# Splitting the opening of an FFT-mixing and GEGLU kernel by residue parity

## Chip, cores, metric

The kernel runs on one core of a Trainium2 chip. The metric is the device time of one execution in microseconds (us), as the median of the runs; lower is better.

## The reference

The input x has 8 batches of 3008 tokens with 256 channels. The first half takes the real part of a two-dimensional Fourier transform over tokens and channels; the second is a gated feed-forward layer with 1536 hidden columns:

```
X = np.fft.fft(x, axis=1); X = np.fft.fft(X, axis=2); a = X.real
g = a @ w_gate                                  # (24064, 1536)
out = (0.5*g*(1 + erf(g/sqrt(2))) * (a @ w_val)) @ w_out   # (24064, 256)
```

## The kernel before

**The transform.** 3008 tokens are 64 x 47. The first stage (`a_step`, 12 steps a batch) multiplies the folded input `xf` by a table `G` of 64-point cosines and sines and copies the result from PSUM to `S1`; its rows are residues. `z_write` puts `S1` into a DRAM tile `z`, `z_read` brings it back as `Ap` with another layout, in three thirds. The second stage (`b_steps`) multiplies 32 slices of `Ap` by 47-point tables (`TP`, `TQ`, and `T0P`, `T0Q` for residue 0) in four groups `q` of eight, once for the even half of the channel transform (`eo` = 0) and once for the odd one (`eo` = 1). `evac` copies a group from PSUM into the token columns `Y`: 1505 columns a batch, since the transform's symmetry gives the other 1503 rows. For batch 0 the odd half runs each step a second time with a one-column weight (`m1`).

The channel transform is folded into the weights: `gen_w` multiplies `w_gate` and `w_val`, cast to bf16 by `cast_w` on POOL, by the table `CW` and copies out `WE`, `WOP` and `WOM` (the odd half with the sign of the mirrored rows). `CW` comes from `phase_c` (POOL), `reduce_c` (DVE) and `sin_c` (ACT).

**Units.** A batch's columns go in three chunks, `CH = [(1024, 481), (0, 512), (512, 512)]`, and each chunk in 12 units of 128 hidden columns: 36 units a batch, 288 in all. A unit multiplies its chunk of `Y` by gate and value weights, for plus and minus rows, applies Gelu on ACT (`glp`, `glm`) and forms the products `h` on DVE (and POOL). In the first chunk of batch 0 (`kind` 0) a unit has six matmuls; from unit 12 on it has five, and DVE makes the minus rows from a broadcast row `nq`, which `n_first` (batch 0) or `n_step` provides. When a chunk's 12 units are done, `l2_steps` multiplies `h` by `Wo_sb` and stores the rows, eight matmuls a unit, beside the next chunk's units.

**Order.** Everything is issued by one loop over units, in program order on each engine's own queue. Inside unit `u` PE runs `val_even(u)`, `gate_minus(u-1)`, `gate_plus(u)` and `val_odd(u-1)`; between them `fill()` pops two matmuls at a time from a list of second-stage steps. DVE's `plus` and minus products follow, then `tail()` empties the second-stage group. After that come the unit's extras (`extra`: `cast_w`, `gen_w`, `gen_wn`), the folds of the next batches on POOL, and the `a_step`s of the next batch (`a_first`: units 4, 5, 8 to 13 for batch 1).

**PSUM.** Of eight banks `ps_g` has two, `ps_v` two pairs, `ps_o` one and `ps_d` one. A new user of `ps_d` waits until the last one's copy is done. `ps_vh` gives half of a `ps_v` pair. In the loop `ps_d` serves `b_steps` of later batches, most `a_step`s, `gen_wn` and some `gen_w`.

**Queues.** All loads, z transfers and stores go through SP's queue in program order; only `load_wo` is on POOL's. In the opening SP has x of batch 0, the first third of the weights, z of batch 0, a small transfer `gate` from z, then the weights for units 4 to 7, x of batch 1 and the weights for units 8 to 11. `warm(n)` issues n matmuls that nothing reads, into `ps_d`; the last eight before the second stage take `gate` as weight, so they start when it lands.

Of the kernel before, what the change touches and what calls it, by code (L numbers as in the profile page):

```python
# [37 lines left out]
def kernel(  # L38
# [34 lines left out]
    CH = [(1024, NCOL - 1024), (0, 512), (512, 512)]  # L73
    MID = 24
# [26 lines left out]
    lone = const_pool.tile([128, NFC], BF16)  # L101

# [92 lines left out]
    def z_tile():  # L195
        return dram.tile([HJ, 128, C], BF16, tag="z", bufs=2, name="z")
# [139 lines left out]
    def sin_g(i):  # L336
        for h in range(2):
            act.activation(
                _sub(G, [[128, 8], [1, 64]], i * 8 * 128 + h * 64),
                _sub(reds[i], [[64, 8], [1, 64]], 0), AF.Sin, scale=col_h[h][:, :])  # L340

    def turn_g():
        for r, to, of, n, sign in ((0, 0, 0, 16, 1.0), (2, 2, 2, 16, -1.0), (1, 1, 33, 8, 1.0),
                                   (1, 33, 1, 8, -1.0), (3, 3, 35, 8, -1.0), (3, 35, 3, 8, 1.0)):
            pat = [[128, 8], [64, 2], [4, n]]
            act.activation(_sub(G, pat, 16 * 128 + to), _sub(G, pat, of), AF.Copy, scale=sign)
# [32 lines left out]
    def reduce_c():  # L379
        for both in redc:  # L380
            reduce_phase(both[:, :C], both[:, C : 2 * C])
        vec.tensor_scalar(col_m, col_p, 1.0, -2.0, op0=ALU.is_ge, op1=ALU.mult)
# [14 lines left out]
    def gen_w(f0, i, eo, bank):  # L397
        fs = slice(f0, f0 + 512)
        ps = bank()
        for t in range(NCH):  # L400
            on_half(ps, pe.matmul(
                ps, CW[:, t, eo, :], _sub(wb[(f0, i)], [[1, 512]], t * 512),
                start=(t == 0), stop=(t == NCH - 1)))
        if eo == 0:
            on_half(ps, act.activation(WE[:, i, fs], ps, AF.Copy))
        else:
            on_half(ps, act.activation(WOP[:, i, fs], ps, AF.Copy))
            on_half(ps, vec.tensor_scalar(
                WOM[:, i, fs], ps, col_m, None, op0=ALU.mult))

# [21 lines left out]
    def n_turn(b):  # L432
        pool.tensor_tensor(
            NA[:, :, :], _sub(Ap, [[0, 2], [C, NG]], 128), TB[:, :, :], op=ALU.mult)
# [46 lines left out]
    def z_write(b, j0, nj, eng=sync):  # L481
        if "z" not in st[b]:
            st[b]["z"] = z_tile()
        z, S1 = st[b]["z"], st[b]["S1"]
        dst = ap_replace(
            z[0:1, 0, :], ap=[[C, 128], [128 * C, nj], [1, C]], offset=z[j0, 0:1, :].offset)
        eng.dma_start(out=dst, in_=_sub(S1, [[C, nj], [1, C]], j0 * C))

    def z_read(b, third):
        z = st[b]["z"]  # L490
        src = ap_replace(
            z[0:1, 0, :], ap=[[NG * C, 32], [1, NG * C]], offset=z[8 * third, 0:1, :].offset)
        p_step = Ap[:, :, :].ap[0][0]
        dst = ap_replace(
            Ap[:, :, :], ap=[[4 * p_step, 32], [1, NG * C]],
            offset=Ap[:, :, :].offset + third * p_step)
        sync.dma_start(out=dst, in_=src)

    def b_steps(b, eo, q):

        box = {}

        def mm(gi, m1):
            def run():
                if "ps" not in box:
                    box["ps"] = ((ps_o, ps_d, ps_vh, ps_vh) if eo else (ps_vh, ps_g) * 2)[q]() \
                        if b == 0 else ps_d()
                ps = box["ps"]
                g = 8 * q + gi
                w = _sub(Ap, [[1, 1 if m1 else 128]], g * C + eo * 128)  # L510
                keep = lambda m: on_half(ps, m)
                even = m1 or eo == 0
                o = gi * N2
                r = slice(0, 1) if m1 else slice(0, 128)
                if g == 0:
                    t = T0P if even else T0Q
                    keep((pe.matmul(
                        ps[r, 0:N2], w, t[:, 0:N2], start=True, stop=True)))
                    keep(pe.matmul(ps[r, 8 * N2 : 8 * N2 + 1], w, t[:, N2 : N2 + 1],
                                         start=True, stop=True))  # L520
                else:
                    s = (36 * g) % N2
                    t = TP if even else TQ
                    keep(pe.matmul(
                        ps[r, o : o + N2], w, t[:, s : s + N2], start=True, stop=True))
            return run

        def copy(o, i):
            if b or q % 2:
                on_half(box["ps"], act.activation(o, i, AF.Copy))  # L530
            else:
                on_half(box["ps"], vec.tensor_copy(o, i))

        def evac_top():
            ps = box["ps"]
            if Ys[b] is None:
                Ys[b] = Y_tile()
            copy(
                _sub(Ys[b], [[32, MID], [1, 8]], eo * YW + 8 * q),
                _sub(ps, [[1, MID], [N2, 8]], 0))  # L540

        def evac_rest():
            if Ys[b] is None:
                Ys[b] = Y_tile()
            ps, Y, g0 = box["ps"], Ys[b], 8 * q
            n2 = N2 - MID
            f = 1 if q == 0 else 0
            copy(
                _sub(Y, [[32, n2], [1, 8 - f]], eo * YW + 32 * MID + g0 + f - 1),
                _sub(ps, [[1, n2], [N2, 8 - f]], MID + f * N2))  # L550
            if q == 0:
                copy(
                    _sub(Y, [[32, n2]], eo * YW + 32 * MID + 31), ps[:, MID:N2])
                copy(
                    _sub(Y, [[1, 1]], eo * YW + NCOL - 1), ps[:, 8 * N2 : 8 * N2 + 1])

        steps = [mm(gi, False) for gi in range(8)]
        if eo == 1 and b == 0:
            steps += [mm(gi, True) for gi in range(8)]
        def evac():  # L560
            evac_rest()
            evac_top()

        return steps, evac, evac_top, evac_rest


# [11 lines left out]
    def open_unit(u):  # L578
# [3 lines left out]
        c0, n = CH[ci]  # L582
# [82 lines left out]

    def windows(b, ci):
        h = hs[(b, ci)]
        c0, n = CH[ci]
# [8 lines left out]
        if len(blocks) % 4:  # L677
            left = blocks[-2:]
            o = 64 * (b % 2)
            pool.tensor_copy(hx[:, :, o : o + 64], h[:, :HXF, 896:960])  # L680
            pool.tensor_copy(_sub(CW, [[128, NCH * 2], [1, 64]], o), h[:, HXF:, 896:960])
            pool.tensor_copy(lone, h[:, :, 960:961])
            if b % 2:
                out.append((None, 0, st[b - 1]["left"] + left, None))
            else:
                st[b]["left"] = left
        return out

    def l2_steps(b, ci):
# [49 lines left out]

        def store_pair(pair, t, queues):  # L740
            ns = len(pair)
            for q in range(4):
# [23 lines left out]
    for i in (1, 0):  # L766
        load_w(0, i)
    phase_g(0)
    phase_g(1)
    cols_c()  # L770
# [3 lines left out]
    pool.tensor_copy(col_k, _sub(reds[1], [[1, 1]], 0))  # L774
    for i in range(3):
        fold_x(0, i, vec, other=pool)
        if i < 2:
            pool.memset(Ap[:, 16 * i : 16 * i + 16, :].bitcast(FP32), 0.0)
        else:
            for t in range(NCH):  # L780
                phase_c(t)
        for k in range(4 * i, 4 * i + 4):
            a_step(0, k)
            if i == 0 and k == 3:
                z_write(0, 0, 8)
            elif i and k % 2:
                z_write(0, 2 * k - 2, 4)
        warm((5, 2, 10)[i])
    z_read(0, 0)
    z_read(0, 1)  # L790
    gate = work.tile([128, 128], BF16, tag="gate", bufs=1, name="gate")
    sync.dma_start(out=gate[:, :], in_=ap_replace(
        st[0]["z"][0:1, 0, :], ap=[[C, 128], [1, 128]], offset=st[0]["z"][0:1, 0, :].offset))
    z_read(0, 2)
    for i in (1, 0):
        load_w(512, i)
    load_x(1, 0)
# [4 lines left out]
    reduce_c()  # L802
    cols_t()
    pt = phase_t()
    sin_c()
    cast_w(0)
# [3 lines left out]
    gen_w(0, 0, 0, ps_g)  # L810
    gen_w(0, 0, 1, ps_vh)
    act.activation(col_f[:, :], col_p[:, :], AF.Gelu)
    warm(4)
    warm(8, gate[:, :])
    later_evacs = []
    for eo in range(2):
        for q in range(4):
            steps, evac, evac_top, evac_rest = b_steps(0, eo, q)
            for s in steps:
                s()  # L820
            if eo:
                evac_rest()
                later_evacs.append(evac_top)
            else:
                evac()
    cast_w(512)
    load_wo()
    extra = {1: [lambda: cast_w(1024)], 13: [gen_tf]}
    for n, turn in ((0, (ps_o, ps_d, ps_o, ps_d)), (1, (ps_o, ps_o, ps_d, ps_o))):
        for j, bank in enumerate(turn):  # L830
            extra.setdefault(4 * n + j, []).append(
# [15 lines left out]
    plan = [first | evens, later | evens]  # L847
    l2q, few = [], False
    for u in range(NU + 2):
# [4 lines left out]
        if u < NU:  # L854
# [4 lines left out]
            if b + 1 < B:  # L859
                for what in plan[min(b, 1)].get(i, ()):  # L860
# [7 lines left out]
                    fills += st[b + 1]["cur"][0][lo:hi]  # L868
# [13 lines left out]
        if u == 0:  # L882
# [8 lines left out]
            n_first(0)  # L891
# [21 lines left out]
        if tail:  # L913
            tail()
        if 0 < u <= NU:
# [29 lines left out]
        if 0 < u <= NU and u % 12 == 0:  # L945
            pb, pi = divmod(u // 12 - 1, 3)
            if CH[pi][0] == 0:
# [34 lines left out]
```

## Time and profile before

| what | value |
|---|---|
| median of 3 runs | 631.36 us (629.62 to 632.13) |
| the profiled execution | 629.75 us |
| its span, first to last instruction | 627.6 us |
| TensorE busy (PE) | 606.0 us, 97% |
| weight loads (PEld), beside PE | 402.0 us, 64% |
| VectorE (DVE) / ScalarE (ACT) / GpSimd (POOL) | 86% / 75% / 72% |
| HBM traffic | 45.08 MB read, 37.25 MB written |

Busy time of PE is that of pipelined matmuls, whose ends are modelled. The waits are inferred from semaphores; the engine named is the one that came last. Line numbers in the profile are those of helpers, so groups are told apart by tile names: `h<-glp,ps_v` is the plus product, `Y<-ps_d` a copy of the second stage, `S<-ps_d` one of the first.

### The profile page before, as it was taken

The page shows a single profiled execution, that of the slowest core. Times are in us where ns is not written, and L with a number is a line of the kernel's source. Part 1 is how long each engine was busy: PE and PEld are TensorE (multiplying, and loading weights), DVE is VectorE, ACT ScalarE, POOL GpSimd, SP SyncE. Part 2 cuts the span into 40 slices and gives each one's busy share as a digit, 9 for nine tenths or more (in the row PEclk, how much of TensorE's full clock was granted, in tenths as well). Part 3 has the DMA queues.
Part 4 walks back from the last instruction along what each step waited for, and adds up shares of the span by engine and source line. Part 5 has one row for each costly group of instructions (what it writes and reads, how often), then busy time and mean ns, then how long its engine had stood idle before and what let it go on. Part 6 is the DMA issues. An engine that isn't in the chain of part 4 may idle for free.

```text
span 627.6 us, 12916 instructions
## 1 busy us (share of the span) xinstructions
PE 606.0 (97%) x4522; PEld 402.0 (64%) x4580; DVE 541.5 (86%) x654; ACT 471.8 (75%) x956; POOL 449.7 (72%) x480
## 2 busy tenths in 40 slices
PE   3899999999999999999999999999999999999997
PEld 2445666766666666766667666666667666666665
DVE  7688988898888998888988898889898898999991
ACT  8687778877788777877778777887778777766662
POOL 8296987769868789687787788687885555556552
PEclk9999999999999999999999999999999999999999
DMA  8997523653237512574246533366223612222113
GB/s 311 348 283 234 153 64 113 173 185 98 76 101 218 194 49 74 177 223 121 51 119 173 190 103 74 104 208 204 56 60 93 194 45 50 60 50 52 39 47 85
DMA packets 65458, 82.39 MB, mean 131 GB/s; under 512 B 8298, under 2 KB 58986, under 8 KB 62578
## 3 DMA queue, kind: packets, MB, share of 16 engines
q1 hardware_dynamic: 63682, 80.65, 42.4%
q0 software_dynamic: 1552, 0.79, 0.9%
q8 instruction: 36, 0.59, 0.4%
q14 instruction: 28, 0.23, 0.1%
q10 hardware_dynamic: 160, 0.13, 0.1%
HBM read 45.08 MB, written 37.25 MB: 131 GB/s over the span
## 4 chain that ended last, share of the span: by engine, by line
PE 91%; DMA 3%; DVE 3%; ACT 1%; issue 1%; POOL 0%; SPq 0%; ACTq 0%; DVEq 0%; POOLq 0%
PE ps_o L25 38%; PE ps_g L25 28%; PE ps_v L25 19%; PE ps_d L25 6%; DMA xin<-in_x_dram 3%; DVE h L25 1%; DVE S L25 0%; DMA z<-S 0%; ACT glp L25 0%; DVE xf L25 0%; ACT glm L25 0%; ACT S L25 0%; POOL xf L25 0%; SPq L25 0%; DVE WOM L25 0%
## 5 line engine op out<-in xcount | busy, mean ns | idle before, releaser
L25 POOL TENSOR_TENSOR h<-glm,dv 128x1024 bf16<-128x1024 bf16 (+1 forms) x138 | 290.9, 2108 | 153.2 <-DVE dv L25 110.0
L25 PE MATMUL ps_o<-Wo_sb,h 128*128 128x256 bf16 x2136 | 277.7, 272 | 0.5 <-DVE S L25 0.3
L25 DVE SCALAR_TENSOR_TENSOR ev<-nq,WN,ps_v 128x512 f32<-128x512 bf16 (+1 forms) x276 | 202.6, 734 | 62.3 <-PE ps_v L25 43.5
L25 ACT ACTIVATE glm<-ps_g 128x512 bf16<-128x512 f32 (+1 forms) x288 | 169.4, 588 | 110.0 <-PE ps_g L25 70.8
L25 PEld LDWEIGHTS <-h 128*128 128x128 bf16 x2208 | 210.8, 97 | 54.6 <-issue 0.9
L25 ACT ACTIVATE glp<-ps_g 128x512 bf16<-128x512 f32 (+1 forms) x288 | 169.9, 590 | 9.9 <-PE ps_g L25 0.3
L25 DVE TENSOR_TENSOR h<-glp,ps_v 128x1024 bf16<-128x1024 bf16 (+2 forms) x150 | 172.9, 1153 | 4.9 <-ACT glp L25 2.7
L25 DVE SCALAR_TENSOR_TENSOR dv<-ev,ps_v 128x1024 f32<-128x1024 f32 (+1 forms) x138 | 164.8, 1194 | 0.0
L25 POOL TENSOR_TENSOR xf<-xin 128x254 bf16<-128x254 f32 x168 | 118.3, 726 | 1.8 <-DMA xin<-in_x_dram 1.8
L25 PE MATMUL ps_g<-Y,WOM 128*128 128x512 bf16 (+1 forms) x288 | 107.7, 374 | 0.3
L25 PE MATMUL ps_v<-Y,WOP 128*128 128x512 bf16 (+1 forms) x288 | 107.7, 374 | 0.0
L25 PE MATMUL ps_v<-Y,WE 128*128 128x512 bf16 (+1 forms) x282 | 105.7, 375 | 0.1
L25 PE MATMUL ps_g<-Y,WOP 128*128 128x512 bf16 (+1 forms) x278 | 103.9, 374 | 1.7
L25 PE MATMUL ps_g<-Y,WE 128*128 128x512 bf16 (+1 forms) x249 | 92.9, 373 | 0.0
L25 PEld LDWEIGHTS <-WOP 128*128 128x128 bf16 x576 | 55.7, 97 | 52.8 <-ACT WOP L25 0.4
L25 PEld LDWEIGHTS <-WE 128*128 128x128 bf16 x576 | 56.0, 97 | 30.9 <-issue 0.6
L25 ACT ACTIVATE osb<-ps_o 128x512 f32<-128x512 f32 x93 | 54.8, 589 | 17.6 <-PE ps_o L25 13.6
L25 PEld LDWEIGHTS <-Ap 128*128 128x128 bf16 (+1 forms) x561 | 40.9, 95 | 33.8 <-issue 0.2
L25 ACT ACTIVATE S<-ps_d 128x512 bf16<-128x512 f32 x80 | 47.4, 593 | 0.1
L25 PEld LDWEIGHTS <-G 128*128 128x128 bf16 x213 | 20.8, 100 | 33.2 <-issue 11.8
L25 ACT ACTIVATE Y<-ps_d 128x192 bf16<-128x192 f32 (+4 forms) x142 | 34.0, 340 | 0.5 <-PE ps_d L25 0.5
L25 PEld LDWEIGHTS <-WOM 128*128 128x128 bf16 x300 | 29.2, 97 | 4.9
(140 smaller groups left out, 262.7 us busy)
## 6 DMA issues: line engine op xcount, KB each, us to landing
out_dram<-osb SPq DMA_DIRECT2D x358, 64.0 KB
xin<-in_x_dram SPq DMA_DIRECT2D x16, 1024.0 KB
Ap<-z SPq DMA_DIRECT2D x24, 512.0 KB
xin<-in_x_dram SPq DMA_DIRECT2D x8, 896.0 KB
z<-S SPq DMA_DIRECT2D x7, 768.0 KB
z<-S SPq DMA_DIRECT2D x8, 512.0 KB
nq<-nrow SPq DMA_DIRECT2D x8, 376.2 KB
z<-S SPq DMA_DIRECT2D x11, 256.0 KB
```

The costliest lines, as they stand in the source:

```text
L25: return lambda *a, **k: self._tc.keep_in_program_order(call(*a, **k))
```

## The change

The rows of `G` are reordered so that even residues stand in partitions 0 to 63 of `S1` and odd ones in 64 to 127. `z` becomes two tiles, one a half; every `z_write` and `z_read` of a batch issues two transfers. In batch 0 the even half is written and read first, and the second stage runs its groups q = 0 and 1 (even residues) alone before unit 0. Groups 2 and 3 run as fills in units 5 to 8. Batch 0 starts with a chunk of 512 columns (even residues of 32 blocks), which needs no odd residue; its rows are stored with stride 2, and a last window of 128 columns is put `aside` until the second chunk. Residue 0 is split over groups 0 and 1, so group 1 has nine steps.

In the opening `reduce_c` goes from DVE to POOL, `phase_c` to the front, two evacuations of `gen_w` from ACT to DVE, two `WOM` products are put off behind them, and the copy of `col_k`, the `gate` transfer and the warm-ups between the first-stage steps go. `gen_w` of units 4 to 7 moves from units 0 to 3 to units 1, 2, 2, 3, `load_wo` to unit 4 and `n_first` to unit 8.

```diff
+    CH0 = [(0, 512), (1024, NCOL - 1024), (512, 512)]
...
     def reduce_c():
         for both in redc:
-            reduce_phase(both[:, :C], both[:, C : 2 * C])
+            ph, tmp = both[:, :C], both[:, C : 2 * C]
+            pool.tensor_scalar(tmp, ph, MAGIC, None, op0=ALU.add)
+            pool.tensor_scalar(tmp, tmp, MAGIC, None, op0=ALU.subtract)
+            pool.tensor_tensor(tmp, tmp, ph, op=ALU.subtract)
...
-        if eo == 0:
-            on_half(ps, act.activation(WE[:, i, fs], ps, AF.Copy))
-        else:
-            on_half(ps, act.activation(WOP[:, i, fs], ps, AF.Copy))
-            on_half(ps, vec.tensor_scalar(
+        copy = act.copy if eng is None else eng.tensor_copy
+        on_half(ps, copy((WE, WOP)[eo][:, i, fs], ps))
+        if eo:
+            minus_two = lambda: on_half(ps, vec.tensor_scalar(
                 WOM[:, i, fs], ps, col_m, None, op0=ALU.mult))
+            if f0:
+                minus_two()
+            else:
+                odd_evacs.append(minus_two)
...
-                    box["ps"] = ((ps_o, ps_d, ps_vh, ps_vh) if eo else (ps_vh, ps_g) * 2)[q]() \
-                        if b == 0 else ps_d()
+                    box["ps"] = ((ps_o, ps_d) if eo else (ps_vh, ps_g))[q]() \
+                        if b == 0 and q < 2 else ps_d()
...
+        def evac_first():
+            if gh:
+                part(0, 32, True)
+            else:
+                part(0, MID, True)
+                part(MID, 32, True)
...
+    cols_c()
+    for t in range(NCH):
+        phase_c(t)
...
             if i == 0 and k == 3:
-                z_write(0, 0, 8)
+                z_write(0, 0, 8, (0,))
             elif i and k % 2:
-                z_write(0, 2 * k - 2, 4)
-        warm((5, 2, 10)[i])
-    z_read(0, 0)
-    z_read(0, 1)
-    gate = work.tile([128, 128], BF16, tag="gate", bufs=1, name="gate")
...
-    z_read(0, 2)
+                z_write(0, 2 * k - 2, 4, (0,))
+                if k == 7:
+                    z_write(0, 0, 8, (1,))
+                elif k == 9:
+                    z_read(0, 0, (0,))
+    warm(7)
+    z_write(0, 8, 8, (1,))
+    z_read(0, 1, (0,))
+    z_read(0, 2, (0,))
     for i in (1, 0):
         load_w(512, i)
+    z_write(0, 16, 8, (1,))
+    for i in range(3):
+        z_read(0, i, (1,))
     load_x(1, 0)
     for i in (1, 0):
         load_w(1024, i)
...
-    gen_w(0, 0, 0, ps_g)
-    gen_w(0, 0, 1, ps_vh)
     act.activation(col_f[:, :], col_p[:, :], AF.Gelu)
-    warm(4)
-    warm(8, gate[:, :])
+    gen_w(0, 0, 0, ps_g, vec)
+    gen_w(0, 0, 1, ps_vh, vec)
+    for w in odd_evacs:
+        w()
+    odd_evacs.clear()
+    warm(6)
...
-    load_wo()
-    extra = {1: [lambda: cast_w(1024)], 13: [gen_tf]}
+    extra = {1: [lambda: cast_w(1024)], 4: [load_wo], 13: [gen_tf]}
...
-            extra.setdefault(4 * n + j, []).append(
+            extra.setdefault(4 + j if n else (1, 2, 2, 3)[j], []).append(
...
+    second_half = {5: (0, 2), 6: (0, 3), 7: (1, 2), 8: (1, 3)}
...
+                if b == 0 and i in second_half:
+                    steps, tail, _, _ = b_steps(0, *second_half[i])
+                    fills += steps
...
-            n_first(0)
...
         if tail:
             tail()
+            if u == 8:
+                n_first(0)
```

## Prediction, on record before the changed kernel ran

> **What bounds the kernel now.** I read the page first: busy times, then the chain that ended last.
>
> ```profile
> PE 606.0 (97%) x4522; PEld 402.0 (64%) x4580; DVE 541.5 (86%) x654; ACT 471.8 (75%) x956; POOL 449.7 (72%) x480
> PE 91%; DMA 3%; DVE 3%; ACT 1%; issue 1%; POOL 0%; SPq 0%; ACTq 0%; DVEq 0%; POOLq 0%
> ```
>
> TensorE (PE) sets the end. What PE must do hardly changes here, so the time moves by what PE waits. The table by stretches (length, then busy time of PE and the other engines) says where it waits:
>
> ```profile
> 0.00:20.00 20.00, 9.84 (x48) 5.19 (x49) 16.34 (x44) 15.24 (x34) 14.76 (x43) 1.00 0.87 299
> 20.00:40.00 20.00, 17.18 (x165) 9.08 (x165) 13.83 (x36) 15.12 (x34) 11.50 (x18) 1.00 1.08 358
> 60.00:80.00 20.00, 19.79 (x151) 12.61 (x153) 18.75 (x21) 14.97 (x33) 19.42 (x22) 1.00 0.54 163
> ```
>
> After 60 us PE is full, so only the opening and units 0 to 11 have time to give. There I read the timeline (start, us, engine, operation).
>
> ```profile
> 16.20 0.91 SPq L25 DMA_DIRECT2D z<-S  x2
> 20.27 1.03 PE L25 MATMUL ps_d<-G 128*128 128x512 bf16 x3
> 23.60 1.90 PE L25 MATMUL ps_d<-G,gate 128*128 128x512 bf16 x8 [2.30 <-DMA gate<-z]
> 25.34 0.19 PE L25 MATMUL ps_v<-T0P,Ap 128*128 128x47 bf16 x2
> 28.60 0.38 PE L25 MATMUL ps_v<-Y,WE 128*128 128x481 bf16 x1
> ```
>
> The first stage goes out through z until 17.1; the second stage starts at 25.34 and unit 0 at 28.60. PE's work in between is filler. Then units 4 and 5:
>
> ```profile
> 37.34 0.65 DVE L25 TENSOR_TENSOR h<-glp,ps_v 128x481 bf16<-128x481 bf16 x1
> 37.48 0.38 PE L25 MATMUL ps_d<-xf,G 128*128 128x256 bf16 x2 [0.42 <-DVE WOM L25]
> 37.70 0.37 PE L25 MATMUL ps_v<-Y,WE 128*128 128x481 bf16 x1
> 37.90 0.65 DVE L25 TENSOR_TENSOR h<-glm,ps_v 128x480 bf16<-128x480 bf16 x1
> 38.47 0.69 DVE L25 CAST S<-ps_d 128x512 bf16<-128x512 f32 x1
> 38.51 0.37 PE L25 MATMUL ps_g<-Y,WOP 128*128 128x481 bf16 x1
> 39.03 0.57 ACT L25 ACTIVATE glp<-ps_g 128x481 bf16<-128x481 f32 x1
> 39.34 0.38 PE L25 MATMUL ps_d<-xf,G 128*128 128x256 bf16 x2
> 39.63 0.66 DVE L25 TENSOR_TENSOR h<-glp,ps_v 128x481 bf16<-128x481 bf16 x1 [0.48 <-ACT glp L25]
> 40.21 0.65 DVE L25 TENSOR_TENSOR h<-glm,ps_v 128x480 bf16<-128x480 bf16 x1
> 40.77 0.74 DVE L25 TENSOR_SCALAR WOM<-ps_o,col_m 128x512 bf16<-128x512 f32 x1
> ```
>
> ps_d is one bank. The step at 37.48 fills it; DVE empties it only at 38.47 to 39.16, behind two products h. A unit's last gate matmul (38.51) is 2.3 us ahead of the moment DVE has finished both products (40.77). Whatever needs ps_d emptied at a unit's end pays that.
>
> **The change, part by part.** The sum is made against the profiled execution: 629.75 us, span 627.6. The median of the runs, 631.36, lies 1.6 above it.
>
> *Opening.* Three warm-up groups between the first-stage steps go; the DVE fold ends at 13.67 as before, so the last S copies end near 15.4 to 16.3 instead of 16.65. The even half of z then needs a last write (3.1 us by the chain's row "16.71 3.11 DMA z<-S") and a read with little queued ahead: 22 to 24, instead of by 25.3. That does not set the start any more. reduce_c moves to POOL and has no row there: nearest are TENSOR_SCALAR 128x127 f32 0.39 and 128x129 0.86, TENSOR_TENSOR 128x254 0.73. For 256 columns I take 2 x 0.39 twice and 0.73, 2.3 per table, 4.5 for two (3.4 to 6.5). From 13.75: CW at 18.3, cast_w's first half (1.04) at 19.3, then gen_w, two copies on ACT (0.5 apart) and three Sin rows (0.36, 0.36, 0.36): 21.7. Then DVE, all in one queue: four T0 pieces at 0.15 apart, two weight copies (0.61 apart), the two WOM products that were put off (0.67 apart), two Y copies: 0.6 + 1.2 + 1.3 + 0.4 = 3.5 to 3.7. Unit 0 starts at 25.4 (24.5 to 27): **-3.2** (-4.1 to -1.6).
>
> At nothing, under this DVE queue: the gate transfer with its 8 matmuls and the copy of col_k go (filler, a wait of POOL's); six warm-up matmuls (6 x 0.21) and the second stage's even half end by 24, while DVE is busy until 25; phase_c on POOL comes ahead of the first cast (four rows, 2.43 together, 5.1 to 7.5), whose result then stands at about 8.5, when DVE's own fold ends at 8.74. If POOL is later than that, the first stage moves, not unit 0.
>
> The first matmuls take 0.43 a pair (8.88 to 10.54), those after the warm-up 0.22. Eight pairs that stay slow would cost 1.7, beside POOL's 4.5: nothing. [...]
>
> *Units 0 to 4.* The first chunk has 512 columns, not 481: six matmuls of 0.216 instead of 0.203, 0.08 a unit. Two of gen_w's ps_d groups now stand in units 2 and 3, one behind the other: 0.2. **+0.6**.
>
> *Units 5 to 8, work.* The odd half's matmuls are only moved. From 25.34 to 28.60, even residues ran 0.026 apart and odd ones with their single-column twins 0.035: 16 x 0.026 + 32 x 0.035 = 1.5, and 0.3 for columns. **+1.9**.
>
> *Units 5 to 8, waits.* All four groups take ps_d, each empties it in the unit's tail, and a_step, gen_w or gen_wn wants it right after. Queued behind PE's wait is the whole next unit, so ACT and DVE dry up too. By the rows:
> - Unit 5: the group's first matmul comes after two of the unit (37.70 + 0.40) and waits for S, 39.16: 1.1. Its tail is two DVE copies (256 and 120 values; rows of 192 take 0.33, of 23 0.25) behind 40.77: until 41.4. a_step(1, 1), which stood at 39.34, waits 2.1.
> - Unit 6: ACT's copy of that step, 0.4; gen_w behind the tail on ACT (two copies behind glp, 0.5 + 0.7 after it starts), 1.1.
> - Unit 7: ACT's copy of WE, 0.4; gen_wn behind a DVE tail as in unit 5, less 0.3 of matmuls still to do: 1.7.
> - Unit 8: a_step(1, 2) behind a tail on ACT: 0.9.
> Sum 7.7, less 0.4 that these units wait already: **+7.3**. The floor is about 2: a tail can't start before glp is done, whatever DVE's queue; the top 9.
>
> *Rest.* Units 9 to 11 carry 0.08 more each, +0.2; the second chunk has 481 columns and five matmuls, -0.8. In later batches the group q = 1 has a ninth step: 14 x 0.03 = **+0.4** (0 to 1.4, by the 0.097 of a bare weight load). There z goes as two DMAs each way: 6 more issues of 0.4 to 0.6 on SP a batch, off the chain: SP sits on it with 0%. The copy of 1536 columns to aside costs POOL about 1.5 (512 take 0.62) in place of three that move to the next chunk (1.2). [...]
>
> *Moved transfers, at nothing.* The weights of unit 8 on (first used in unit 4) come behind z's rest: x lands about 31, and cast_w's first half, 34.3 before, meets unit 4's gen_w at about 34. Cover is thin; without it, 1. n_first moves from unit 0 to 8 and has four units. load_wo moves from 28.73 to about 40; landing took 15.2, so 56 at worst, and its first matmul stood at 53.30. The waits above hide that; without them it costs up to 2.7.
>
> Sum: -3.2 + 0.6 + 1.9 + 7.3 + 0.2 - 0.8 + 0.4 = **+6.4**: 636.2 on the profiled execution, 637.8 on the median. I name 637.0, between them.
>
> **Rivals.**
> *The waits do not come* (slower turns to not slower): each tail would have to end within 0.8 us of the last gate matmul, so that the next step finds ps_d empty. For it: DVE idles 0.5 before some products. Against: 38.51 to 40.77. Then 6.4 - 7.3 = -0.9: 630 on the median's base, 629.5 at the best opening. Chance 0.12.
> *Half of the waits*: PE's lateness lets DVE catch up and products end sooner. +2.8: 634. Chance 0.18.
> *The even half is not earlier* (the change does not do what it says): the reads queue behind the odd writes, or POOL's reduce takes 6.5. Then unit 0 starts at 27 or later: +8 to +9.6, 640. For it: z's transfers ran at only 220 to 300 GB/s from 14 to 20 us. Chance 0.12.
> The forecast keeps 0.58, with 634 to 640 for itself.
>
> **How the numbers follow.** 0.5% is 3.2 us, about what a measurement of this kernel can tell from no change. Nearly all of the forecast, 0.55, the third rival, 0.12, and a third of the second, 0.06, are slower: 0.73. Faster needs the first rival and 2 us that no row shows: 0.06. The rest, 0.21, is the same. The range runs from 630.5 (most of the first rival left out) to 641.
>
> **What would show it.** Right: unit 0's first 512-column matmul at 24.5 to 27; in units 5 and 7, PE waiting 1.5 to 2 for ps_d released by DVE Y copies, in 6 and 8 about 1 by ACT's; unit 12 six to eight us later than before (its first matmul stood near 51.6). Wrong: ps_d waits in these units under 3 together, a start before 24, or PE below its 19.8 of 20 after 60 us.

## Result: 15 us slower; the trace agrees with the forecast in the middle and not at its start

The changed kernel takes 646.33 us (645.57 to 650.39, 4 runs) against 631.44 us (629.62 to 632.13): ratio 1.0253, 95% interval 1.0206 to 1.0301. The forecast was 637.0, with a range to 641.0: slower, as it said, but by 15 us, where it had 6. The profiled execution took 646.56 us, its span is 644.5, 16.9 us longer than before.

The page of the changed kernel, its busy times and its chain:

```profile
PE 611.3 (95%) x4581; PEld 402.5 (62%) x4581; DVE 547.5 (85%) x652; ACT 482.1 (75%) x942; POOL 457.7 (71%) x485
PE 89%; POOL 4%; DMA 3%; DVE 1%; ACT 1%; SPq 1%; issue 0%; POOLq 0%; ACTq 0%
```

TensorE still sets the end, but POOL has come onto the chain, from 0% to 4% (about 26 us). The stretches (length, then PE, PEld, DVE, ACT, POOL, granted clock, DMA share, GB/s):

```profile
0.00:20.00 20.00, 5.94 (x28) 3.38 (x29) 14.32 (x31) 18.65 (x30) 18.74 (x45) 1.00 0.58 215
20.00:40.00 20.00, 13.79 (x103) 6.62 (x101) 13.43 (x37) 11.91 (x28) 5.32 (x6) 0.91 0.88 261
60.00:80.00 20.00, 18.69 (x107) 10.93 (x108) 17.03 (x23) 13.35 (x26) 8.47 (x15) 0.88 0.61 179
```

In the first 20 us PE does 5.94 where it did 9.84, while ACT and POOL are busier than before. The last row holds a second surprise: the clock is 0.88 after 60 us. From 80 to 620 us PE is busy 540.0 of 540 us (537.0 before): the steady part adds no time.

The opening, from the timeline (start, us, engine, operation):

```profile
4.85 9.52 ACT L25 ACTIVATE G<-dv,col_h 128x512 bf16<-128x512 f32 x4 [0.46 <-DVE dv L25]
15.64 0.58 ACT L25 ACTIVATE S<-ps_g 128x512 bf16<-128x512 f32 x1
5.05 6.14 POOL L25 TENSOR_SCALAR red<-dv,col_c 128x129 f32<-128x129 f32 x4
11.14 1.29 POOL L25 CAST xf<-xin 128x16 bf16<-128x16 f32 x1
12.48 0.58 PE L25 MATMUL ps_g<-xf,G 128*128 128x256 bf16 x2 [12.48 <-POOL xf L25]
30.03 0.19 PE L25 MATMUL ps_v<-T0P,Ap 128*128 128x24 bf16 x2 [4.34 <-DMA Ap<-z]
32.18 0.61 PE L25 MATMUL ps_v<-Y,WE 128*128 128x512 bf16 x1
```

Two steps that the prediction had at no cost stand here. ACT's four Sin instructions over `G` take 9.52 us in all, 2763 ns each with their ends overlapping; the group before was

```profile
L25 ACT ACTIVATE G<-dv,col_h 128x512 bf16<-128x512 f32 x4 | 2.7, 714 | 0.5 <-DVE dv L25 0.5
```

that is, 714 ns each. The first copies of S stand behind them on ACT's queue. And `phase_c` on POOL takes 6.14 where the prediction had 2.43, so the first cast of x starts at 11.14 (6.41 before) and the first matmul at 12.48 (8.88 before). Both stand ahead of the first stage. Its first copy of S starts at 15.64, z's even half lands for the second stage at 30.03, and unit 0 starts at 32.18, where 24.5 to 27 was forecast.

Unit 5, for the rows of before at 37.34 to 40.77:

```profile
45.58 0.38 PE L25 MATMUL ps_g<-Y,WOP 128*128 128x512 bf16 x1
46.62 0.69 DVE L25 TENSOR_TENSOR h<-glp,ps_v 128x512 bf16<-128x512 bf16 x1 [1.68 <-ACT glp L25]
47.23 0.68 DVE L25 TENSOR_TENSOR h<-glm,ps_v 128x512 bf16<-128x512 bf16 x1
47.82 0.61 DVE L25 CAST Y<-ps_d 128x256 bf16<-128x256 f32 x2
48.58 0.38 PE L25 MATMUL ps_d<-xf,G 128*128 128x256 bf16 x2 [1.93 <-DVE Y L25]
```

This is the chain that the prediction drew: two products, then the tail's two copies, then the step that wanted ps_d, 1.93 us late (forecast: 2.1).

Where the time went, by the start of a unit's first matmul in both traces:

| stretch | before | after | difference | forecast |
|---|---|---|---|---|
| start of unit 0 | 28.60 | 32.18 | +3.6 | -3.2 |
| units 0 to 4 | 9.10 | 11.87 | +2.8 | +0.6 |
| units 5 to 8 | 7.86 | 17.52 | +9.7 | +9.2 |
| units 9 to 12 | 8.61 | 9.96 | +1.35 | +0.2 |
| the rest: spans, 16.9, less the 17.4 above | | | -0.5 | -0.4 |

Of the 10.5 us that the forecast missed, 6.8 are the opening and 2.2 units 0 to 4.

### The profile page after: what moved, and what is told of

The parts are those of the page before. It is cut to its first block, busy times and chain, and to the rows that moved or that the text cites. A ratio compares the mean times of both kernels' runs of the same rounds, so it can differ in the third digit from the quotient of the medians.

```text
span 644.5 us, 13001 instructions
## 1 busy us (share of the span) xinstructions
PE 611.3 (95%) x4581; PEld 402.5 (62%) x4581; DVE 547.5 (85%) x652; ACT 482.1 (75%) x942; POOL 457.7 (71%) x485
## 4 chain that ended last, share of the span: by engine, by line
PE 89%; POOL 4%; DMA 3%; DVE 1%; ACT 1%; SPq 1%; issue 0%; POOLq 0%; ACTq 0%
PE ps_o L25 37%; PE ps_g L25 28%; PE ps_v L25 18%; PE ps_d L25 6%; POOL red L25 2%; DMA z<-S 1%; DMA xin<-in_x_dram 1%; DVE h L25 1%; POOL Ap L25 1%; POOL xf L25 1%; SPq L826 0%; SPq L25 0%; ACT glp L25 0%; POOL wb L25 0%; DVE S L25 0%
## 5 line engine op out<-in xcount | busy, mean ns | idle before, releaser
L25 PE MATMUL ps_v<-Y,WE 128*128 128x512 bf16 (+1 forms) x288 | 108.6, 377 | 0.0
L25 PE MATMUL ps_g<-Y,WOP 128*128 128x512 bf16 (+1 forms) x288 | 108.4, 376 | 0.0
L25 PE MATMUL ps_g<-Y,WE 128*128 128x512 bf16 (+1 forms) x288 | 108.3, 376 | 0.0
L25 PEld LDWEIGHTS <-Ap 128*128 128x128 bf16 (+1 forms) x578 | 44.4, 97 | 44.4 <-issue 7.7
L25 ACT ACTIVATE Y<-ps_d 128x192 bf16<-128x192 f32 (+4 forms) x133 | 41.5, 409 | 1.5 <-PE ps_d L25 1.5
L25 PE MATMUL ps_d<-xf,G 128*128 128x256 bf16 x162 | 31.6, 277 | 2.7 <-DVE Y L25 1.9
```

The lines of the kernel that those rows point to most:

```text
L25: return lambda *a, **k: self._tc.keep_in_program_order(call(*a, **k))
```

## Experiments

Theory: the opening is late for two reasons, the order in which Sin writes `G` and the place of `phase_c`; what lies between units 5 and 8 are the waits for ps_d that the prediction priced. The rivals were that the late opening comes from z in halves, from POOL's `reduce_c` or from the order on SP's queue, and that the loss in units 5 to 8 is DVE shut out by POOL, or the clock. All kernels are edits of the changed one. The table gives the result of each and the starts of four units in its trace. Each ratio is to the kernel before as it ran beside that kernel, with medians from 629.75 to 631.61 us, so kernels from different rows are better compared by their ratios than by their times.

| kernel | us | ratio to before, 95% interval | unit 0 | unit 5 | unit 9 | unit 13 |
|---|---|---|---|---|---|---|
| before | 631.44 | | 28.60 | 37.70 | 45.56 | 54.17 |
| changed | 646.33 | 1.0253 (1.0206 to 1.0301) | 32.18 | 44.05 | 61.57 | 71.53 |
| e1_sin_order | 644.38 | 1.0223 (1.0184 to 1.0261) | 29.23 | 44.00 | 62.55 | 71.47 |
| e2_phase_late | 647.20 | 1.0264 (1.0229 to 1.0300) | 32.04 | 43.42 | 63.13 | 73.09 |
| e3_both | 640.53 | 1.0165 (1.0139 to 1.0191) | 28.12 | 37.33 | 55.27 | 64.18 |
| e4_tail_early | 648.70 | 1.0296 (1.0266 to 1.0325) | 31.81 | 43.83 | 63.40 | 73.29 |
| e5_order | 639.27 | 1.0148 (1.0128 to 1.0168) | 28.53 | 37.93 | 55.24 | 64.16 |
| e6_tail_wn | 635.66 | 1.0088 (1.0064 to 1.0113) | 28.46 | 38.59 | 52.24 | 61.15 |
| e7_all | 635.84 | 1.0092 (1.0072 to 1.0112) | 28.08 | 37.29 | 51.67 | 60.58 |
| e8_all_dve | 633.76 | 1.0066 (1.0040 to 1.0092) | 25.99 | 35.93 | 50.26 | 59.18 |
| e9_wn_act | 645.66 | 1.0244 (1.0221 to 1.0266) | 32.26 | 43.70 | 62.03 | 71.99 |
| e10_mended | 632.70 | 1.0031 (1.0019 to 1.0043) | 25.95 | 35.22 | 46.03 | 56.44 |
| e11_odd_opening | 634.91 | 1.0069 (1.0052 to 1.0086) | 31.84 | 41.54 | 49.89 | 59.38 |
| e12_tails_as_after | 638.51 | 1.0115 (1.0093 to 1.0136) | 25.76 | 35.04 | 53.35 | 63.62 |

### The order of Sin's writes

```diff
-                _sub(G, [[128, 8], [1, 32], [64, 2]], i * 8 * 128 + h * 32),
-                _sub(reds[i], [[64, 8], [2, 32], [1, 2]], 0), AF.Sin, scale=col_h[h][:, :])
+                _sub(G, [[128, 8], [64, 2], [1, 32]], i * 8 * 128 + h * 32),
+                _sub(reds[i], [[64, 8], [1, 2], [2, 32]], 0), AF.Sin, scale=col_h[h][:, :])
```

The same values go to the same places; only the order changes, from pairs that lie 64 elements apart to runs of 32. The input, read in one run before, is then read in steps of two.

> The changed kernel with the two loops of the Sin over G swapped (the same elements, written in runs of 32 neighbours instead of pairs 64 apart). Theory A (the write pattern makes the Sin slow): each of the four Sin instructions takes about 0.7 us again instead of 2.8, the last S copy ends near 18 instead of 20.6, unit 0 starts near 29.7 instead of 32.2, and the time falls by about 2.5 us against the changed kernel. Theory B (POOL's phase_c, which now runs beside it, slows it): the Sin stays above 2 us, the time stays within 1 us.

The group of Sin in this kernel:

```profile
L25 ACT ACTIVATE G<-dv,col_h 128x512 bf16<-128x512 f32 x4 | 2.8, 749 | 0.5 <-DVE dv L25 0.5
```

749 ns, against 2763 in the changed kernel: the order was nearly the whole of it, and since the reads became the less regular ones, it is the order of the writes. Unit 0 starts at 29.23, 2.95 earlier. But unit 5 starts at 44.00, where it was, and the time falls by a difference that the intervals do not separate. The timeline says where the gain went:

```profile
42.76 1.01 PE L25 MATMUL ps_o<-wb,CW 128*128 128x512 bf16 x2 [4.80 <-POOL wb L25]
```

Unit 4's `gen_w` waits 4.80 us for POOL's cast of its weights (1.86 in the changed kernel). On POOL that cast stands behind the first fold of batch 1, which started at 40.20, and x for that fold was issued on SP at 32.00, behind the odd half of z. This is the cover that the prediction called thin.

### phase_c behind the casts, alone and with the Sin order

```diff
     cols_c()
-    for t in range(NCH):
-        phase_c(t)
...
+        else:
+            for t in range(NCH):
+                phase_c(t)
```

> The changed kernel with phase_c back behind the last fold's cast. Theory A: the Sin stays at 2.8 us, POOL's first cast comes at 6.4 again and the first matmul at about 8.9, but the S copies still wait for ACT until about 15.7 and POOL's chain to CW is 2.4 longer: unit 0 between 31 and 33.5, time within 1.5 us of the changed kernel. Theory B: the Sin falls back to 0.7 and unit 0 starts before 29.5, 3 us or more less. On phase_c itself: if the DVE folds slow it, its four instructions take 2.4 in all behind them, not 6.1.

> Both edits together. If the slow Sin and the early phase_c are the two causes of the late opening: first matmul at 8.9, last S copy near 16.5, reduce_c on POOL from 15 to 20, unit 0 at 26 to 28.5 instead of 32.2, the time 4 to 6 us under the changed kernel and still some 10 above the kernel before, the waits in units 5 to 8 unchanged. If the z transfers are the cause (the second stage waited 4.3 us for Ap): unit 0 stays above 30.

`phase_c` alone, behind the third cast, takes 2.43 again, and the first matmul comes at 9.84, but it does not help: Sin now holds it.

```profile
9.84 0.61 PE L25 MATMUL ps_g<-xf,G 128*128 128x256 bf16 x2 [9.84 <-ACT G L25]
14.47 0.61 PE L25 MATMUL ps_g<-xf,G 128*128 128x256 bf16 x2 [2.75 <-ACT G L25]
```

Unit 0 starts at 32.04. With both edits the first matmul starts at 8.71 (8.88 before), unit 0 at 28.12 and unit 5 at 37.33; the time is 640.53, nearly 6 us less.

```profile
28.12 0.39 PE L25 MATMUL ps_v<-Y,WE 128*128 128x512 bf16 x1 [0.71 <-DVE Y L25]
```

At unit 0 the order of Sin is worth 2.95 alone, the place of `phase_c` 0.14 alone, and both together 4.06. In the time neither shows alone: what the one still holds, or the next holder behind the first stage, takes the gain. Units 0 to 4 now take 9.21, as before (9.10): the wait for the weights went with the late z, not by an edit of its own.

### Tails ahead of the products

```diff
-            if b or q % 2:
+            if b or q == 1:
...
+        early_tail = b == 0 and i in second_half and u < NU
-        def fill(most=2):
+        def fill(most=None):
+            most = most or (4 if early_tail else 2)
...
+            if early_tail:
+                while fills:
+                    fill()
+                tail()
...
         if tail:
-            tail()
+            if not early_tail:
+                tail()
```

The odd groups are done four matmuls at a time, and DVE empties all of them ahead of the products.

> The changed kernel with the odd groups' steps popped four at a time and their copies all on DVE, issued ahead of the unit's plus product instead of behind both products. Theory (ps_d is emptied too late): PE's waits for ps_d in units 5 to 8 fall from about 5 us to under 1.5, units 5 to 8 take 12 to 13.5 us instead of 17.5, the slow clock after unit 8 goes too, the time falls by 5 to 6.5 us. Rival (DVE has no time left in these units): the products come later by what the copies take, the wait shows up at ps_v or ps_g, and the time falls by under 2 us.

Units 5, 6 and 7 take 4.06, 2.69 and 3.73 instead of 4.75, 3.39 and 5.01, as the waits would have it, but unit 8 takes 9.09, and the kernel is no faster. DVE and PE there:

```profile
55.53 6.33 DVE L25 CAST WN<-WNb 128x12 f32<-128x12 bf16 x1
61.77 0.68 DVE L25 CAST Y<-ps_d 128x256 bf16<-128x256 f32 x2
62.60 0.59 PE L25 MATMUL ps_d<-xf,G 128*128 128x256 bf16 x2 [5.23 <-DVE Y L25]
```

A copy of 12 values, from SBUF to SBUF, takes 6.33 us and ends when POOL's run of folds does (61.8); the tail stands behind it, and PE waits 5.23 us for the tail. So the expected gain did not come. In the changed kernel the same copy took 4.44, in the kernel before 0.53:

```profile
57.59 4.44 DVE L25 CAST WN<-WNb 128x12 f32<-128x12 bf16 x1
```

```profile
45.09 0.53 DVE L25 CAST WN<-WNb 128x12 f32<-128x12 bf16 x1
```

That raises the question whether this copy, and not ps_d, was the loss in units 5 to 8. e9_wn_act is the changed kernel with this copy on ACT alone (`vec.tensor_copy` becomes `act.copy`):

> The changed kernel with only the copy WN (12 values) on ACT instead of DVE. In the changed kernel it sat on DVE from 57.6 to 62.0, in unit 8. If it is on the path: it takes 0.2 us, unit 8 is 1 to 2 us shorter than 4.4, and the time falls by 1 to 3 us. If unit 8 is set by ps_d and the slow clock alone: within 0.7 us of the changed kernel.

On ACT it takes 0.20 us, and the time stays (1.0244 against 1.0253, intervals over each other); units 5 to 8 take 18.33. So in the changed kernel the copy cost nothing that can be told: in its trace unit 8 is held by its own matmuls, at a granted clock of 0.50, and by ACT's tail (a wait of 0.74). The copy decides only where a tail is queued behind it.

### The order on SP, and all of it together

Four kernels on e3_both: e5_order puts x of batch 1 and the weights from unit 8 on ahead of the odd half of z; e6_tail_wn adds the early tails and WN's copy on ACT; e7_all has both; e8_all_dve gives `reduce_c` back to DVE as well.

```diff
-    z_write(0, 16, 8, (1,))
-    for i in range(3):
-        z_read(0, i, (1,))
     load_x(1, 0)
     for i in (1, 0):
         load_w(1024, i)
+    z_write(0, 16, 8, (1,))
+    for i in range(3):
+        z_read(0, i, (1,))
```

> e3_both with x and the weights of batch 1's first loads queued on SP ahead of the odd half's rest of z (its last write and three reads). Theory C (the odd half's z holds up the loads behind it): POOL's folds of batch 1 start near 27.5 instead of 33.9, and end before unit 8. In e3 no unit waits for them any more, so by that alone the time stays within 1 us. Theory D (DVE's copy WN of 12 values, 2.6 us in e3 and 4.4 in the changed kernel against 0.5 before, waits for POOL's unbroken run of folds): the copy takes under 0.7 and the time falls by about 2 us against e3.

> e3_both with the early tails of e4 and the copy WN on ACT instead of DVE. Theory (ps_d is emptied too late, and in e4 a WN copy of 6.3 us took the gain back): units 5 to 8 take 12.5 to 14.5 us instead of 17.9, no wait above 1.5 us is left there, the time falls 3.5 to 5 us below e3. Rival (DVE has no time left): under 1.5 us.

> e6_tail_wn with the order of e5. If the transfers do not bind once the waits are mended: within 1 us of e6. If they do, because the units are now ahead of the loads: 1 to 3 us less than e6.

> e7_all with reduce_c back on DVE. If POOL's chain phase_c, reduce_c, cast_w sets the opening (it ends at 22.4 in e3): cast_w ends near 17.5, unit 0 starts at 24.8 to 26.5 instead of 28.1, the time falls by 1.5 to 3 us against e7, and is still 1 to 4 us above the kernel before. If the even half's z sets it: unit 0 stays above 27.

The order is worth nothing that can be told: e5_order against e3_both, and e7_all against e6_tail_wn, lie within each other's intervals, and unit 13 starts at 64.16 and 64.18 in the first pair. The folds start at 29.77 instead of 33.91, but nothing waits for them. WN's copy takes 0.17 us in e5_order, as theory D had it, but the 2 us that it was to give do not come. The early tails, together with WN's copy on ACT, are worth 4.9 us (e6_tail_wn against e3_both). `reduce_c` on DVE is worth 2.1 us between the medians and at the start of unit 0 (e8_all_dve against e7_all); the two ratios' intervals overlap, and unit 13 starts 1.4 earlier. In that kernel the opening is the one that the prediction described, but for the engine of `reduce_c`:

```profile
23.54 0.19 PE L25 MATMUL ps_v<-T0P,Ap 128*128 128x24 bf16 x2 [2.07 <-DMA Ap<-z]
25.99 0.61 PE L25 MATMUL ps_v<-Y,WE 128*128 128x512 bf16 x1 [0.38 <-DVE Y L25]
```

z lands at 23.54 (forecast 22 to 24), and unit 0 waits for DVE's copies of Y and starts at 25.99 (forecast 25.4, 24.5 to 27). z in halves is thus no hindrance to the even half.

### The odd half back in the opening

e11_odd_opening is e8_all_dve with groups 2 and 3 of both halves ahead of unit 0, as in the kernel before, their z right behind the even one's, and `n_first` back in unit 0:

```diff
-        for q in range(2):
+        for q in range(4):
...
-    second_half = {5: (0, 2), 6: (0, 3), 7: (1, 2), 8: (1, 3)}
+    second_half = {}
```

> e8_all_dve with the odd half back in the opening: its z right behind the even half's, groups 2 and 3 before unit 0, nothing in units 5 to 8. If the price lies in units 5 to 8: unit 0 starts at 28 to 29.5, 2 to 3.5 later than in e8, units 5 to 8 take 8 to 9 us instead of 14.3, and the time is 2 to 4 us under e8, within 1.5 us of the kernel before. If it lies in the new chunk order, the halved z or the strided stores of the whole run: it stays 2 or more above the kernel before.

The expectation was missed: it takes as long as e8_all_dve. Units 5 to 8 fall from 14.33 to 8.35, so their work and waits were worth 6.0; but unit 0 starts 5.85 later.

```profile
27.80 0.48 PE L25 MATMUL ps_v<-TP,Ap 128*128 128x47 bf16 x8 [2.86 <-DMA Ap<-z]
```

The odd half of z is there at 27.80, 3.5 behind the even one (24.34), where before all of it served at 25.34; and in the windows from 25 to 35 us the clock is 0.59 and 0.73. Between these two kernels the parity opening is a trade: what it takes out of the opening it puts into units 5 to 8, at the same price; part of that price in e11_odd_opening is the slower clock, and in its queue the odd half is later than the whole was. The rival (chunk order, halved z, strided stores) had its sign too, since the time is 4.3 above the kernel before. But of the 5.6 us between the spans of the two profiled executions 5.2 lie ahead of unit 13; all that comes behind it, the strided stores and the halved z of later batches among it, adds 0.4.

### The two last kernels

e10_mended is e8_all_dve with four edits that aim at the waits left: no step of the second stage ahead of a unit's gate matmuls, the S copy of batch 1's first step on ACT, `gen_wn` in unit 9, sixteen warm-up matmuls instead of six.

> e8_all_dve with four more edits for the waits that it has left: no odd step before the gate matmuls, the S copy of a_step(1, 0) on ACT, gen_wn in unit 9 instead of 7, and 16 warm-up matmuls instead of 6 before the second stage. By the sum (the odd half's work of 1.9 us is only moved, the opening gives 2.6): units 5 to 8 take 11 to 12.5 us instead of 14.3, units 0 and 1 take 0.21 us a matmul instead of 0.43, the time falls by 2 to 3.5 us below e8 and ends within 1.5 us of the kernel before, not below it by more than 0.5. Rival (the split is worth its 3 us once it is well fitted in): 1 us or more under the kernel before.

Units 5 to 8 take 10.81 instead of 14.33, a little less than expected, and the clock stays at 1.00 in every window of 5 us up to 70. But units 9 to 12, where `gen_wn` went, take 10.41 instead of 8.92, and the time falls by 1.1 (2.2 by the ratios), at the low end of the 2 to 3.5 expected or under it. It is 632.70, ratio 1.0031 (1.0019 to 1.0043): the best version of the change, still 2.1 above the median of the kernel before beside it, where 1.5 at most was expected. The four edits were not run one by one.

e12_tails_as_after is e8_all_dve without the early tails: an opening at the time that the prediction assumed (with `reduce_c` on DVE), with the waits that it priced.

```diff
-            if b or q == 1:
+            if b or q % 2:
...
-        early_tail = b == 0 and i in second_half and u < NU
-
-        def fill(most=None):
-            most = most or (4 if early_tail else 2)
+        def fill(most=2):
...
-            if early_tail:
-                while fills:
-                    fill()
-                tail()
...
-            if not early_tail:
-                tail()
+            tail()
```

> All of the opening mended (order of the Sin writes, phase_c behind the casts, reduce_c on DVE, x and weights ahead of the odd half's z), WN's copy on ACT, but the tails of units 5 to 8 as the change has them: copies behind the products, two steps a pop. This is the opening that the prediction assumed, with the waits that it priced. My theory (with the opening right, the units 5 to 8 cost what the forecast said): unit 0 at 25.5 to 26.5, units 5 to 8 together 17.0 to 18.0 us (7.86 in the kernel before), with the waits for ps_d released by DVE's and ACT's copies of Y between 5 and 6.5 in sum, and a time of 636 to 638, ratio 1.009 to 1.013. Rival (with an earlier start, POOL's and DVE's work lies otherwise and most of these waits go): units 5 to 8 at 15 or less, ps_d waits under 3, a time within 1 us of 633.8, that of the kernel with early tails.

638.51 us, ratio 1.0115 (1.0093 to 1.0136): half a microsecond over the 636 to 638 expected, inside the ratio's bounds. Unit 0 starts at 25.76; units 5 to 8 take 18.31, where 17 to 18 were expected. Of it 5.1 are waits behind copies of Y (5 to 6.5 expected), each within 0.02 us of the same wait in the changed kernel (1.94 and 1.52 behind DVE's, 0.89 and 0.75 behind ACT's). The rival, that most of them go with an earlier start, falls. Beside them stands a wait of 1.48 for `Ap` in unit 5; e5_order and e8_all_dve, with the same order of transfers but unit 5 later (37.93 and 35.93 for 35.04), wait there 1.37 and 1.30 behind DVE's copy of S instead. And the windows show the clock (e12_tails_as_after first, then e8_all_dve):

```profile
35.00:50.00 15.00, 8.54 (x87) 4.15 (x88) 8.27 (x16) 6.91 (x14) 14.85 (x29) 1.00 1.01 276
50.00:57.00 7.00, 6.25 (x33) 3.00 (x32) 2.62 (x5) 4.06 (x8) 2.38 (x6) 0.54 0.17 55
```

```profile
35.00:50.00 15.00, 11.54 (x112) 5.52 (x111) 10.48 (x22) 8.49 (x16) 14.98 (x29) 1.00 1.01 276
50.00:57.00 7.00, 6.50 (x38) 3.37 (x37) 5.71 (x11) 5.50 (x11) 2.48 (x6) 1.00 0.34 94
```

With PE busy 8.54 of 15 us the clock then fell to 0.54; with 11.54 of 15 it did not. The share of busy time alone did not decide, though: the changed kernel's clock fell after 9.33 busy of 15, and in e5_order, with waits of the same size, PE was busy 8.81 of the 15 us from 37 to 52, and its matmuls of 512 columns went on taking 0.38 us each up to 62 (0.60 to 0.63 in the changed kernel's slow stretch).

## Why the prediction was wrong, and where it was right

**Opening, -3.2: wrong by 6.8.** This is the step that failed, and on two things that the prediction put at nothing. The reordering of `G` was read as a change of places: the sum has no term for its Sin rows, and they went from 0.71 to 2.76 us (0.75 in e1_sin_order). And `phase_c` was moved "at nothing" with its old 2.43; at its new place it took 6.14 (the rows of 127 values 2124 ns for 386), beside DVE's folds of x, and the cast that it stands ahead of came 4.7 later. The trace of before held a sign of it: of the two rows of 129 values, which the prediction read by their mean of 0.86, one took 1.34 beside the last of DVE's folds and the other 0.38 behind it. The prediction added that a late POOL would move the first stage and not unit 0; e1_sin_order, where only `phase_c` is early, starts unit 0 1.1 later than e3_both, so it moves both.

Both together are 4.1 of the 6.8 (e3_both starts unit 0 at 28.12), and 2.1 more come back with `reduce_c` on DVE. The price of `reduce_c` on POOL was right, 2.4 a table (0.86, 0.86, 0.72; forecast 2.3), with some luck, since it came from rows of another shape. Its place was not: with `phase_c` behind the casts it runs from 14.82 to 20.04 in e3_both (13.75 to 18.3 in the forecast), and three of the four pairs of `gen_w`'s matmuls behind it take 1.01 to 1.06 us instead of 0.59. With everything mended unit 0 starts at 25.8 to 26.0 for 25.4, but that needed `reduce_c` on DVE; a start at 25.4 was not to be had with it on POOL in any order that was run.

**Units 0 to 4, +0.6: wrong by 2.2,** by way of the opening. 1.86 are unit 4's wait for cast weights: "cover is thin; without it, 1" had the right place and half of the size. e3_both shows no such wait with the order on SP as it was, so the moved transfers were hidden once z was in time. The rest goes with the clock: it was 0.50 from 32 to 34 us, and unit 0's first two matmuls are 0.40 apart instead of 0.216.

**Units 5 to 8, +9.2: right in sum, +9.7.** The waits came where they were put, behind the copies that were named. From the changed kernel's trace, in order: 0.35 and 1.93 in unit 5 (forecast 1.1 and 2.1), 0.25 and 0.88 in unit 6 (0.4 and 1.1), 0.24 and 1.51 in unit 7 (0.4 and 1.7), 0.74 in unit 8 (0.9): 5.9 for 7.7. What made up for it is the clock, which fell to 0.50 at 57.9, within unit 8. So the sum here is right by luck: the waits were 1.8 too dear, and a slow clock that was not in the sum took their place. The cleaner test is e5_order, where unit 4 does not wait and the matmuls of 512 columns take 0.38 us each in these units (0.60 to 0.63 in the changed kernel's slow stretch): units 5 to 8 take 17.31, +9.45 for +9.2, with waits of 6.9 for 7.7. Putting the tails back late costs 3.1 us by the ratios of e12_tails_as_after and e8_all_dve (4.75 between their medians, 4.4 at unit 13), which shows that the waits and what hangs on them were the price. The rival "waits do not come" falls.

**Units 9 to 12, +0.2: +1.35,** all but the forecast part of it in the stretch of slow clock, which lasts until about 64.6. The sum has no term for a slow clock behind the opening, and that is the step that failed here. **The rest, -0.4: right** (-0.5): the gain of the second chunk, the ninth step of later batches and the doubled z transfers come to what was forecast in sum, though not one by one, and no wait for `Wo_sb` shows.

**The signs.** Those for the waits came (1.93 and 1.51 behind DVE's Y in units 5 and 7, 0.88 and 0.74 behind ACT's). Unit 0 at 32.18 was outside 24.5 to 27, PE's 18.69 of 20 after 60 us was named as a sign of error and was one, and unit 12 came 17 us later, not six to eight.

**The rivals.** "The even half is not earlier" is the one that came, with its price too small: it had unit 0 at 27 to 28.6, and its causes (reads behind the odd writes, a reduce of 6.5 on POOL) were not those that acted. It was to come in place of the forecast's opening, by 640; nothing in the list reached 646, since each rival kept the other terms at their forecast size. With the opening about as assumed, e12_tails_as_after puts the whole sum to the test: +6.4 forecast, +6.9 measured between the medians, but +8.9 between the spans of the profiled executions, on which the sum was made. By the traces the opening gives 2.8 (3.2 forecast), units 5 to 8 cost 10.5 (9.2) and units 9 to 12 1.7 (0.2), in both with a slow clock (0.54 from 50 to 57 us) that the prediction had left out.

## What to carry to other kernels

When a table's layout changes, price the instruction that writes it anew by the order of its writes (here 0.71 us became 2.76), and when an instruction moves, look up who runs on the neighbouring engine at its new place: here the old trace's rows, 2.43 us, were the price only in the old place, and the new one's was 6.14. Before moving work out of a stretch where an engine waits, count what the banks it needs are doing where it goes: here six microseconds out of the opening were six into units 5 to 8. And a gain at the start was worth only the distance to the next holder behind it: e1_sin_order won 3 us at unit 0 and had lost all of it at unit 5.

## What the runs showed of the hardware

**Writes in pairs.** ACT's Sin over 128x512 bf16 took 0.71 us with runs of 64 elements, 0.75 with runs of 32 (and reads in steps of two), and 2.76 when two consecutive elements lay 64 elements (128 bytes) apart. That is 3.7 times the time with runs of 32; why such writes cost more is not shown.

**POOL beside DVE.** POOL's operation on 128x127 f32 took 386 ns behind DVE's folds of x (the kernel before, first line) and 2124 ns beside them (the changed kernel):

```profile
L25 POOL TENSOR_SCALAR red<-dv,col_c 128x127 f32<-128x127 f32 x2 | 0.8, 386 | 0.0
L25 POOL TENSOR_SCALAR red<-dv,col_c 128x127 f32<-128x127 f32 x2 | 4.2, 2124 | 0.0
```

It was as slow in e1_sin_order (2122), with ACT's Sin short, and as fast in e2_phase_late (379), with the Sin still long, so ACT's Sin is not what slowed it. That DVE's folds did is read from the times: both slow ones end 0.17 us behind a fold (7.53 and 11.19, the folds at 7.36 and 11.02).

The other way round, DVE's copy of 12 values from SBUF to SBUF took 2.63 us in e3_both, 4.44 in the changed kernel and 6.33 in e4_tail_early, and each time ended within 0.05 us of the last fold of POOL's run. In e5_order, where the folds started at 29.77 instead of e3_both's 33.91, it took 0.17. But in the kernel before it took 0.53 and ended at 45.62, with one fold (45.59), while POOL's run went on to 51.7. That POOL's folds shut it out is read from these coincidences; it was not tried with the folds taken away, and why it got in between two folds in the one kernel and not in the others is not shown.

**The clock after waits of up to 1.93 us.** In the changed kernel the granted clock fell to 0.50 at 57.9 us, and matmuls went from 0.216 to 0.43 us apart until about 64.6. PE had waited 1.93 us at the longest since 40 us, and it had been busy 5.61 of the 10 us up to 50, and 9.33 of the 15 up to 57.9:

```profile
40.00:50.00 10.00, 5.61 (x38) 2.43 (x36) 6.20 (x11) 4.57 (x8) 9.13 (x15) 1.00 0.74 298
57.60:64.60 7.00, 6.25 (x34) 2.91 (x33) 6.22 (x5) 3.64 (x7) 4.53 (x10) 0.52 0.21 52
```

That these waits brought the slow clock is read from the order of the two, and no run here shows where the border lies: the clock fell in e12_tails_as_after (8.54 busy of 15 us, then 0.54), it did not in e8_all_dve (11.54, then 1.00), and in e5_order (8.81) the matmuls of 512 columns went on taking 0.38 us.
